# Row maxima split by VectorE before their transposition, which ordinary products make ahead of the values products

## The chip, the core and the metric

The kernel runs on one core of a Trainium2 chip. Its engines are TensorE (PE in the profile; PEld are its weight loads), VectorE (DVE), ScalarE (ACT), GpSimd (POOL) and SyncE (SP), which here issues all transfers. The metric is the device time of one execution in microseconds (us).

## The reference

One transformer block on 2048 positions of width 512, with conditioning: a normalised and modulated input goes through attention with 32 heads of 16 numbers each, then a normalised and modulated sum goes through two dense layers with the Mish function between them.

```python
mod = (_silu(c) @ w_mod).reshape(c.shape[0], 6, 1, -1)
sa, ca, ga, sb, cb, gb = ...
h = _layernorm(x) * (1 + ca) + sa
    qkv = (h @ wqkv) ...                                  # 32 heads of 16
    p = _softmax(einsum("bhqd,bhkd->bhqk", q, k) * 16 ** -0.5)
    o = einsum("bhqk,bhkd->bhqd", p, v)
x = x + ga * (o @ wo)
h = _layernorm(x) * (1 + cb) + sb
x = x + gb * (mish(h @ w1 + b1) @ w2)
```

The softmax is the part that matters here: each score is reduced by the largest one of its row before the exponential.

## The kernel before

**Blocks and steps.** Attention is cut into 32 blocks, n = 0 to 31: 512 queries by 4 heads. A block has 16 steps, each with 128 keys of the 4 heads; the program's step t belongs to block t // 16. In step t, ScalarE needs scores with the keys along the partitions, so the row maxima (along the keys) can't be taken from them. They are found by a second set of products with the queries along the partitions, 20 steps ahead: in step t the maxima of step t + 20 (`PRO`).

**A step.** TensorE makes 4 products for maxima (L471) and 4 for scores (L512), in turn. Each lands in a bank of PSUM of a *ring* of six banks, handed out in order by `ring()`; so the seventh product has to wait until the first one's bank has been read. VectorE reads a maxima product with one reduction (L473, tile `mx`), ScalarE a score product with one exponential (L520, tile `pr`). Products use half of TensorE's rows; the other half makes, beside them, products of the remaining work (L132: projections, and the two dense layers of the query rows that are done already). Then `pv(t - 2)` multiplies the exponentials of two steps before with the values (L540, four products, each in two passes, eight records). Between its exponentials ScalarE also does stages of the dense layers, such as L758, a logarithm of the Mish function.

**The maxima's way.** After the last maxima of a block, in step 16n - 5, `neg_max` reduces them (L482, tile `mm`; each value is written twice, into neighbouring groups of columns). At the end of step 16n - 4, behind that step's values products, `max_rows` takes two neighbouring banks of the ring with `ring(2)`, transposes the two halves of `mm` into them (L490, one transposition for each half of the partitions), and VectorE makes two parts of each value, from PSUM: `mh` (L494) is the value times -1, rounded to TensorE's short type, and `mt` (L495) holds that, or what the rounding left over, according to a column `lows` of 0 and -1. In the middle of the next step SyncE copies `mt` into two further rows of the query tiles `qa` (L501); the key tiles hold ones there, so that the score products come out less their row's maximum.

**Order.** No scheduler moves anything: the order on each engine is the order in which the code of `step` issues. Hooks run work at given half steps; `ats[t]` holds functions that are called at the end of step t, `max_rows` among them. Waits between engines come from what an instruction reads and writes; for the ring they are kept per bank.

Of the kernel before, what the change touches and what calls it, by code (L numbers as in the profile page):

```python
# [8 lines left out]
F32 = mybir.dt.float32  # L9
F32R = mybir.dt.float32r  # L10
AF = mybir.ActivationFunctionType
ALU = mybir.AluOpType
AX = mybir.AxisListType
# [5 lines left out]
def adaln_block(ctx: ExitStack, tc: tile.TileContext, x, wqkv, wo, w1, b1, w2, c, w_mod, out):  # L19
    nc = tc.nc  # L20
    P = 128
# [17 lines left out]
    PRO = 16 + LEAD  # L39
# [7 lines left out]
    out = out[0]  # L47
# [3 lines left out]
    cst = ctx.enter_context(tc.tile_pool(name="cst", bufs=1))  # L51
# [11 lines left out]
    ident = cst.tile([P, P], F32, name="ident")  # L63
# [10 lines left out]
    nc.gpsimd.memset(sel, 0.0)  # L74
    for k in range(DK):
        nc.gpsimd.memset(sel[32 * k:32 * k + 1, :], 1.0)
    lows = cst.tile([P, 1], F32, name="lows")
    nc.vector.tensor_reduce(out=lows[:32], in_=ident[:32, :32].rearrange("p (a v q) -> p v a q", a=4, v=2)[:, 1], op=ALU.add,
                            axis=AX.XY)
    nc.vector.tensor_scalar_mul(lows[:32], lows[:32], -1.0)  # L80
    modc = cst.tile([P, 4, DK], F32, name="modc")
    sil = cst.tile([P, DK], F32, name="sil")
    b1c = cst.tile([P, FT], F32, name="b1c")
# [63 lines left out]
    def ring(w=1):  # L147
        if w == 2 and ring_at[0] % 2:
            ring_at[0] += 1
        b = ring_at[0] % NRING  # L150
        ring_at[0] += w
        return ring_t[:, b, :] if w == 1 else ring_t[:, b:b + 2, :]

    def bank(tag="ms"):
        return ring() if tag == "ring" else ps.tile([P, TB], F32, tag=tag, name="bk", bufs=1)
# [29 lines left out]
    def at(h, f):  # L185

        hooks.setdefault(h, []).append(f)
# [122 lines left out]
    with ExitStack() as es:  # L310
# [69 lines left out]
        for i in range(2):  # L380
            pr.append(ring())
            for k in range(DK):
                nc.tensor.matmul(pr[i][32 * k:32 * k + 32, :], sil[:, k:k + 1].to_broadcast([P, 32]), wma[i][:, k, :],
                                 start=True, stop=True)
# [33 lines left out]
        for tb in range(NB):  # L418
# [4 lines left out]
            parts = []  # L423
# [28 lines left out]
    ap = ctx.enter_context(tc.tile_pool(name="ap", bufs=1, reuse_waits="tile"))  # L452
# [5 lines left out]
        nc.sync.dma_start(t, vscr[n % G])  # L458
        vgs[n] = t

    mxs = {}

    def max_tile(n, j, s, qs, kb):

# [12 lines left out]
    def neg_max(n):  # L477

        mx = mxs.pop(n)
        mm = ap.tile([P, 4, 2, 4], F32, tag="mm", name="mm", bufs=2)  # L480
        twice = bass.AP(tensor=mx.tensor, offset=mx.offset, ap=[list(mx.ap)[0], [16, 4], [0, 2], [4, 4], [1, 4]])
        nc.vector.tensor_reduce(out=mm, in_=twice, op=ALU.max, axis=AX.X)  # L482
        ats.setdefault(16 * n + 16 - PRO, []).append(lambda: max_rows(n, mm))

    def max_rows(n, mm):
        t = ring(2)
        cols = mm.rearrange("p a v q -> p (a v q)")
        for g in range(2):
            r = slice(64 * g, 64 * g + 64)
            nc.tensor.transpose(t[:32, g, :64], cols[r], ident[r, r])  # L490
        pt = t[:32, :, :64]
        mh, mt = [ap.tile([32, P], F32R, tag=n_, name=n_, bufs=1) for n_ in ("mh", "mt")]
        halves = [m.rearrange("p (g q) -> p g q", g=2) for m in (mh, mt)]
        nc.vector.tensor_scalar_mul(halves[0], pt, -1.0)  # L494
        nc.vector.scalar_tensor_tensor(halves[1], halves[0].bitcast(F32), lows[:32], pt, op0=ALU.mult, op1=ALU.subtract)  # L495

        def put():
            for j in range(2):
                for s in range(2):
                    o = (2 * s + j) * 8  # L500
                    nc.sync.dma_start(  # L501
                        qa[(2 * n + j) % NR][64 * s + 48:64 * s + 50, :].rearrange("v (s q) -> v s q", s=4).bitcast(F32),
                        mt[o:o + 8, :].bitcast(F32))
        at(2 * (16 * n + 16 - PRO) + 3, put)
# [27 lines left out]
    def pv(t):  # L532
        if not 0 <= t < T:
            return
        n, kc = divmod(t, 16)
        if kc == 0:
            accs[n] = bank("acc")
        for h in range(4):
            o = (kc * 4 + h) * VW
            nc.tensor.matmul(accs[n][32 * h:32 * h + 32, :], vgs[n][:, o:o + 32], pts.pop((t, h)),  # L540
                             start=(kc == 0), stop=(kc == 15))
        if kc == 15:
            evac(n)

    o_hl = {}
    st, mst = {}, {}

    def evac(n):
        qb, g = divmod(n, G)
# [538 lines left out]
    ats = {}  # L1088
# [47 lines left out]
    def maxima(n, u, s, others):  # L1136

        j, qs = divmod(u, 4)
        return ([max_tile(n, j, s, qs, kb) for kb in range(4 - others)],
                [max_tile(n, j, 1 - s, qs, kb) for kb in range(4 - others, 4)])  # L1140

    def step(t):
        second = t % 2
        n, u = t // 16, t % 16 // 2
        tm = t + PRO
        run_hooks(2 * t)
        if t < 0:

            for i in range(2):
                if tm < 16:  # L1150
                    kb, jq = divmod(2 * tm + i, 8)
                else:
                    jq, kb = tm % 16 // 2, 2 * second + i
                for s in range(2):
                    max_tile(tm // 16, jq // 4, s, jq % 4, kb)()
            if second and tm % 16 == 15:
                neg_max(tm // 16)
            run_hooks(2 * t + 1)
            for f in ats.pop(t, []):
                f()  # L1160
            whole_units(2 * t + 1, CREDIT)
            do_specials(2 * t + 1)
            return
        s = 0 if second else 1
        own, others = ([score(n, j, v, 2 * u + i) for i in range(2) for j in range(2)] for v in (s, 1 - s))
        if not second and 1 < t < T:
            next_part(2 * t)
        part = list(cur["part"])
        f = len(part)
        if t >= T:  # L1170
            if t == T:
                cur["tag"] = "acc"
            run_hooks(2 * t + 1)
            pv(t - 2)
            whole_units(2 * t + 1, 8)
            do_specials(2 * t + 1)
            return
        swap, held = False, None
        if tm < T:
            o = max(0, (8 - f) // 2)  # L1180
            mo, alone = maxima(tm // 16, tm % 16 // 2, s, o)

            mine = [x for p in zip(mo, own) for x in p] + own[len(mo):]
            kinds = [k for p in zip("m" * len(mo), "s" * len(mo)) for k in p] + ["s"] * (len(own) - len(mo))
            swap = 2 <= f <= len(mine) and kinds[f - 1] == "s" and kinds[f - 2] == "m"
            if swap:
                mine[f - 2:f] = mine[f - 1], mine[f - 2]
        else:
            o = max(0, (4 - f) // 2)
            mine = own[o:] if second else own[:4 - o]  # L1190
            alone = others[4 - o:] if second else others[:o]

            m = len(mine)
            if f > m:
                mine = [mine[(i * m) // f] if (i + 1) * m // f > i * m // f else None for i in range(f)]
        beside = part + alone

        def emit(product):
            e = product()
            if cur.pop("want", None):  # L1200
                cur["after"] = e

        ends = second and f and not cur["left"]
        for i in range(max(len(mine), len(beside))):
            if i == len(mine) // 2:
                run_hooks(2 * t + 1)
            if i < f:
                last = i + 1 == f
                if i < len(mine) and mine[i] and not last:
                    if swap and ends and i + 2 == f:  # L1210
                        held = mine[i](True)
                    else:
                        emit(mine[i])
                for m in beside[i]:
                    mm_half(m, second, cur["first"], bool(ends and last and m is beside[i][-1]),
                            cur.pop("after", None))
                    cur["first"] = False
                if last:
                    if ends:
                        cur["fin"](2 * t + 2)  # L1220
                        cur["fin"] = None
                    if held:
                        held()
                    cur["want"] = True
                    if i < len(mine) and mine[i]:
                        emit(mine[i])
            else:
                for x in (*mine[i:i + 1], *beside[i:i + 1]):
                    emit(x)
        if tm < T and tm % 16 == 15:  # L1230
            neg_max(tm // 16)
        do_specials(2 * t + 1)
        pv(t - 2)
        for f in ats.pop(t, []):
            f()

    def do_specials(h):
        if specials and h >= specials[0][0]():
            fin = specials.pop(0)[1]()
            pe_run()  # L1240
            at(h + 1, lambda: fin(h + 1))
# [90 lines left out]
    def run_hooks(h):  # L1332
        while h in hooks:
            for f in hooks.pop(h):
                f()
# [4 lines left out]
    t = T + 2  # L1340
# [32 lines left out]
```

## Time and profile before

| | before |
|---|---|
| median of 3 runs | 1696.65 us (1695.23 to 1700.46) |
| profiled execution | 1693.26 us, span 1691.5 us |
| granted TensorE clock | 0.996 |
| TensorE / VectorE / ScalarE busy | 98% / 85% / 78% |
| transpositions L490 | 64, 228 ns each |
| VectorE L482, L494, L495 | 32 each, 286, 279 and 335 ns |

Busy time is a union of records; a matmul's record reaches to its modelled end, so two that follow each other overlap. In the timeline a row begins with its start and its length in us; what stands in brackets at its end is the idle time of its engine before it, and what ended that. Line numbers are those of the kernel before; from `neg_max` on, the changed kernel's are higher by one (L513 for L512, L521 for L520, L541 for L540), except where the change itself stands.

### The profile page before, as it was taken

What the parts mean: (1) busy time and instruction counts of PE and PEld (TensorE: products, weight loads), DVE (VectorE), ACT (ScalarE), POOL (GpSimd) and SP (SyncE); (2) the same over time, 40 slices, a digit from 0 to 9 for tenths busy, and PEclk for the clock granted to TensorE, in tenths of its full rate; (3) what the DMA queues carried; (4) which work ended last, traced back from release to release, by engine and by line L of the source; (5) the groups of instructions that cost most, each with busy time, mean ns of one, the idle gap of its engine ahead of it and who ended that gap; (6) DMA issues with size and microseconds to landing.
All of it is one profiled execution on the core that took longest, in us unless ns stands there. A gap on an engine that the chain in (4) does not pass through costs nothing.

```text
span 1691.5 us, 32962 instructions
## 1 busy us (share of the span) xinstructions
PE 1660.6 (98%) x12316; PEld 921.7 (54%) x12316; DVE 1429.9 (85%) x2362; ACT 1327.1 (78%) x2559; POOL 898.0 (53%) x906
## 2 busy tenths in 40 slices
PE   6999999999999999999999999999999999999998
PEld 5755665554435455555555555555555555554687
DVE  6898898887998888988888888889888888881577
ACT  6247777777778898888889898888888898889264
POOL 5155215565504388755525498654535597646432
PEclk9999999999999999999999999999999999999999
DMA  7767457777772342434353644334442535332362
GB/s 249 192 224 215 120 159 213 250 226 226 232 210 63 111 123 74 127 80 149 86 133 74 197 105 99 99 109 123 117 103 79 176 95 131 93 107 82 132 218 74
DMA packets 113992, 240.03 MB, mean 142 GB/s; under 512 B 24048, under 2 KB 49648, under 8 KB 107784
## 3 DMA queue, kind: packets, MB, share of 16 engines
q1 hardware_dynamic: 113832, 237.92, 49.6%
q8 instruction: 97, 1.59, 0.4%
q14 instruction: 63, 0.52, 0.1%
HBM read 179.95 MB, written 51.44 MB: 137 GB/s over the span
## 4 chain that ended last, share of the span: by engine, by line
PE 92%; DVE 3%; DMA 2%; ACT 2%; SPq 1%; issue 1%; POOL 0%; DVEq 0%; ACTq 0%; POOLq 0%
PE bk L540 30%; PE ring L471 23%; PE ring L512 22%; PE bk L132 9%; PE bk L126 3%; PE ring L126 3%; PE ring L1074 2%; DVE mx L473 1%; ACT pr L520 1%; DMA xt<-in_A_x 1%; SPq L318 0%; DMA qa<-mt 0%; PE bk L1006 0%; DMA vg<-vscr 0%; PE ring L842 0%
## 5 line engine op out<-in xcount | busy, mean ns | idle before, releaser
L473 DVE TENSOR_REDUCE mx<-ring 128x1 f32<-128x512 f32 x2048 | 1276.1, 684 | 161.5 <-PE bk L132 104.9
L520 ACT ACTIVATE pr<-ring 128x512 f32<-128x512 f32 x2048 | 1090.2, 605 | 232.0 <-PE bk L132 168.8
L471 PE MATMUL ring<-ka,qa 64*128 64x512 f32 x2048 | 778.7, 427 | 0.5
L512 PE MATMUL ring<-qa,ka 64*128 64x512 f32 x2048 | 723.0, 397 | 7.8 <-ACT pr L520 4.6
L471 PEld LDWEIGHTS ring<-ka,qa 64*128 64x128 f32 x2048 | 366.5, 184 | 407.9 <-DVE mx L473 356.2
L540 PE MATMUL bk<-pr,vg 128*32 128x512 f32 x4096 | 545.9, 605 | 0.0
L512 PEld LDWEIGHTS ring<-qa,ka 64*128 64x128 f32 x2048 | 374.1, 184 | 120.8 <-ACT pr L520 35.6
L132 PE MATMUL bk<-h,w 64*128 64x512 f32 x1008 | 280.7, 410 | 0.0
L132 PE MATMUL bk<-w,a_h 64*128 64x512 f32 x576 | 194.8, 417 | 0.6 <-ACT pr L520 0.4
L132 PEld LDWEIGHTS bk<-h,w 64*128 64x128 f32 x1008 | 171.5, 184 | 5.7 <-ACT pr L520 0.4
L540 PEld LDWEIGHTS bk<-pr,vg 128*32 128x32 f32 x4096 | 81.0, 108 | 125.1 <-issue 117.0
L740 POOL TENSOR_SCALAR ee<-hb 128x512 f32<-128x512 f32 x42 | 62.5, 1488 | 96.7 <-ACT hb L734 88.2
L132 PE MATMUL bk<-w,a_l 64*128 64x512 f32 x288 | 113.7, 395 | 0.0
L770 POOL TENSOR_TENSOR ee<-ee,rr 128x512 f32<-128x512 f32 x42 | 53.9, 1284 | 111.6 <-ACT rr L761 111.4
L132 PEld LDWEIGHTS bk<-w,a_h 64*128 64x128 f32 x576 | 95.3, 185 | 5.2 <-ACT pr L520 1.5
L132 PE MATMUL bk<-w,o_hl 64*128 64x512 f32 x288 | 79.7, 409 | 0.0
L98 POOL TENSOR_TENSOR a_l<-hb,a_h 128x512 fp32r<-128x512 f32 x53 | 71.7, 1354 | 4.4
L893 POOL TENSOR_TENSOR y<-yd,y 128x512 f32<-128x512 f32 x40 | 51.4, 1285 | 35.5 <-ACT yd L892 35.3
L754 POOL TENSOR_SCALAR rr<-ee 128x512 f32<-128x512 f32 x42 | 26.1, 622 | 60.0 <-ACT ee L746 59.9
L132 PE MATMUL bk<-h_h,wl 64*128 64x512 f32 x168 | 57.5, 423 | 0.0
L95 POOL TENSOR_SCALAR a_h<-hb 128x512 fp32r<-128x512 f32 x53 | 36.3, 684 | 39.9 <-DVE hb L768 38.3
L774 POOL TENSOR_TENSOR hb<-hb,rr 128x512 f32<-128x512 f32 x42 | 54.5, 1298 | 3.3
(205 smaller groups left out, 1840.9 us busy)
## 6 DMA issues: line engine op xcount, KB each, us to landing
ka<-kscr SPq DMA_DIRECT2D x124, 384.0 KB
w<-w2scr SPq DMA_DIRECT2D x56, 512.0 KB
w<-w1scr SPq DMA_DIRECT2D x46, 512.0 KB
vg<-vscr SPq DMA_DIRECT2D x32, 552.0 KB
qa<-qscr SPq DMA_DIRECT2D x124, 100.0 KB
kscr<-qh SPq DMA_DIRECT2D x16, 512.0 KB
qscr<-qh SPq DMA_DIRECT2D x32, 256.0 KB
hl<-in_B_w SPq DMA_DIRECT2D x28, 256.0 KB
```

Source lines behind the costliest of these rows:

```text
L98: (nc.gpsimd if eng == "p" else nc.vector).tensor_sub(lo, src, hi.bitcast(F32))
L126: nc.tensor.matmul(acc, l, r, start=start, stop=stop)
L132: i = nc.tensor.matmul(acc, l[64 * g:64 * g + 64], r[64 * g:64 * g + 64], start=start, stop=stop)
L471: nc.tensor.matmul(pm, qt[64 * s:64 * s + 64, qs * P:(qs + 1) * P], kt[64 * s:64 * s + 64, kb * TB:(kb + 1) * TB], start=True, stop=True)
L473: return nc.vector.tensor_reduce(out=mxs[n][:, s, 4 * j + qs, kb:kb + 1], in_=pm, op=ALU.max, axis=AX.X)
L512: nc.tensor.matmul(p_, kt[64 * s:64 * s + 64, kc * P:(kc + 1) * P], qt[64 * s:64 * s + 64, :], start=True, stop=True)
L520: e = nc.scalar.activation(pr, p_, AF.Exp, scale=SCALE)
L540: nc.tensor.matmul(accs[n][32 * h:32 * h + 32, :], vgs[n][:, o:o + 32], pts.pop((t, h)), start=(kc == 0), stop=(kc == 15))
L740: nc.gpsimd.tensor_scalar_min(buf("ee", 2), b["hb"], HCAP)
L770: nc.gpsimd.tensor_mul(ee, ee, rr)
L774: nc.gpsimd.tensor_mul(hb, hb, rr)
L893: nc.gpsimd.tensor_add(y[i], yd, y[i])
```

## The change

- `neg_max` reduces to each value once (`mm` is half as large) and splits it at once on VectorE, ahead of the transposition: the value times -1, rounded, and what the rounding left over go into neighbouring groups of columns of a tile `mhl`, whose first 32 columns are used; the other 96 are set to zero once.
- `max_rows` makes two ordinary products of `mhl` (all 128 columns as weights) with a unit matrix `eyes` of the short type, where two transpositions were, and ScalarE copies the result into `mt`; VectorE has nothing more to do with it.
- `max_rows` is called from a list of its own, `ahead`: in step 16n - 4 as before, but in front of `pv(t - 2)`.

```diff
-    lows = cst.tile([P, 1], F32, name="lows")
...
+    eyes = cst.tile([P, P // 2], F32R, name="eyes")
+    for g in range(2):
+        r = slice(64 * g, 64 * g + 64)
+        nc.vector.tensor_copy(eyes[r], ident[r, r])
...
     def neg_max(n):
 
         mx = mxs.pop(n)
-        mm = ap.tile([P, 4, 2, 4], F32, tag="mm", name="mm", bufs=2)
-        twice = bass.AP(tensor=mx.tensor, offset=mx.offset, ap=[list(mx.ap)[0], [16, 4], [0, 2], [4, 4], [1, 4]])
-        nc.vector.tensor_reduce(out=mm, in_=twice, op=ALU.max, axis=AX.X)
-        ats.setdefault(16 * n + 16 - PRO, []).append(lambda: max_rows(n, mm))
-
-    def max_rows(n, mm):
+        mm = ap.tile([P, 4, 4], F32, tag="mm", name="mm", bufs=2)
+        nc.vector.tensor_reduce(out=mm, in_=mx.rearrange("p s (j q) b -> p (s j) q b", j=2), op=ALU.max, axis=AX.X)
+        if "mhl" not in st:
+            st["mhl"] = ap.tile([P, P], F32R, tag="mhl", name="mhl", bufs=1)
+            nc.vector.tensor_scalar_mul(st["mhl"], ident, 0.0)
+        parts = st["mhl"][:, :32].rearrange("p (a v q) -> p a v q", a=4, v=2)
+        nc.vector.tensor_scalar_mul(parts[:, :, 0], mm, -1.0)
+        nc.vector.scalar_tensor_tensor(parts[:, :, 1], parts[:, :, 0].bitcast(F32), -1.0, mm, op0=ALU.mult, op1=ALU.subtract)
+        ahead.setdefault(16 * n + 16 - PRO, []).append(lambda: max_rows(n))
+
+    def max_rows(n):
         t = ring(2)
-        cols = mm.rearrange("p a v q -> p (a v q)")
         for g in range(2):
             r = slice(64 * g, 64 * g + 64)
-            nc.tensor.transpose(t[:32, g, :64], cols[r], ident[r, r])
-        pt = t[:32, :, :64]
-        mh, mt = [ap.tile([32, P], F32R, tag=n_, name=n_, bufs=1) for n_ in ("mh", "mt")]
-        halves = [m.rearrange("p (g q) -> p g q", g=2) for m in (mh, mt)]
-        nc.vector.tensor_scalar_mul(halves[0], pt, -1.0)
-        nc.vector.scalar_tensor_tensor(halves[1], halves[0].bitcast(F32), lows[:32], pt, op0=ALU.mult, op1=ALU.subtract)
+            nc.tensor.matmul(t[:, g, :64], st["mhl"][r], eyes[r], start=True, stop=True)
+        mt = ap.tile([32, P], F32R, tag="mt", name="mt", bufs=1)
+        nc.scalar.copy(mt.rearrange("p (g q) -> p g q", g=2), t[:32, :, :64])
...
         do_specials(2 * t + 1)
+        for f in ahead.pop(t, []):
+            f()
         pv(t - 2)
         for f in ats.pop(t, []):
             f()
```

In the steps before the first (t < 0), which have no values products, `ahead` is called where `ats` was.

TensorE at the end of step 16n - 4, block 12, before: the last three products of the step, the four values products (L540), the two transpositions (L490), and the first products of the next step.

```order
L471 MATMUL ring<-ka_105,qa_107 128x512
L512 MATMUL ring<-qa_109,ka_634 128x512
L471 MATMUL ring<-ka_105,qa_107 128x512
L540 MATMUL bk<-pr_0_1175,vg 32x512
L540 MATMUL bk<-pr_2_1151,vg 32x512
L540 MATMUL bk<-pr_0_1182,vg 32x512
L540 MATMUL bk<-pr_2_1159,vg 32x512
L490 MATMUL ring<-ident,mm 32x64 x2
L471 MATMUL ring<-ka_105,qa_107 128x512
L132 MATMUL bk<-h_5831,w_6934 128x512
```

The same place now (L494 are the two products with the unit matrix, L541 the values products):

```order
L471 MATMUL ring<-ka_105,qa_107 128x512
L513 MATMUL ring<-qa_109,ka_634 128x512
L471 MATMUL ring<-ka_105,qa_107 128x512
L494 MATMUL ring<-eyes,mhl 128x64 x2
L541 MATMUL bk<-pr_0_1177,vg 32x512
L541 MATMUL bk<-pr_2_1153,vg 32x512
L541 MATMUL bk<-pr_0_1184,vg 32x512
L541 MATMUL bk<-pr_2_1161,vg 32x512
L471 MATMUL ring<-ka_105,qa_107 128x512
L132 MATMUL bk<-h_5833,w_6936 128x512
```

The pair has gone past the four values products and follows the step's last product directly; it fills 128 partitions instead of 32.

VectorE around the same border, before: the reduction of `mx` to `mm`, the four maxima of step 16n - 4, then the two parts.

```order
L473 TENSOR_REDUCE mx<-ring 128x1 x20
L482 TENSOR_REDUCE mm<-mx 128x32
L473 TENSOR_REDUCE mx<-ring 128x1 x4
L494 TENSOR_SCALAR mh<-ring 32x128
L495 SCALAR_TENSOR_TENSOR mt<-mh,lows,ring 32x128
L473 TENSOR_REDUCE mx<-ring 128x1 x40
```

The same place now:

```order
L473 TENSOR_REDUCE mx<-ring 128x1 x20
L481 TENSOR_REDUCE mm<-mx 128x16
L486 TENSOR_SCALAR mhl<-mm 128x4x4
L487 SCALAR_TENSOR_TENSOR mhl<-mhl,mm 128x4x4
L473 TENSOR_REDUCE mx<-ring 128x1 x44
```

Three operations now stand in front of the four maxima of step 16n - 4, and none behind them.

ScalarE there, now: the exponentials of step 16n - 4 (L521) with a stage of the Mish function (L759) between the first and the second, the copy into `mt` (L496), and two exponentials of the next step.

```order
L521 ACTIVATE pr_0_1151<-ring 128x512
L759 ACTIVATE rr<-ee,two 128x512
L521 ACTIVATE pr_0_1159<-ring 128x512
L521 ACTIVATE pr_1_1152<-ring 128x512
L521 ACTIVATE pr_1_1160<-ring 128x512
L496 CAST mt<-ring 32x128
L521 ACTIVATE pr_2_1179<-ring 128x512
L521 ACTIVATE pr_2_1186<-ring 128x512
```

The copy is new on this engine and stands behind the step's last exponential; the others have kept their order.

More of the change, by code (lines that the diff above doesn't have):

```diff
@@ L76, in adaln_block @@
         nc.gpsimd.memset(sel[32 * k:32 * k + 1, :], 1.0)
-    lows = cst.tile([P, 1], F32, name="lows")
-    nc.vector.tensor_reduce(out=lows[:32], in_=ident[:32, :32].rearrange("p (a v q) -> p v a q", a=4, v=2)[:, 1], op=ALU.add,
-                            axis=AX.XY)
-    nc.vector.tensor_scalar_mul(lows[:32], lows[:32], -1.0)
+    eyes = cst.tile([P, P // 2], F32R, name="eyes")
+    for g in range(2):
+        r = slice(64 * g, 64 * g + 64)
+        nc.vector.tensor_copy(eyes[r], ident[r, r])
     modc = cst.tile([P, 4, DK], F32, name="modc")
@@ L459, in load_v @@
         vgs[n] = t
-    mxs = {}
+    mxs, st, ahead = {}, {}, {}
     def max_tile(n, j, s, qs, kb):
@@ L545, in adaln_block @@
     o_hl = {}
-    st, mst = {}, {}
+    mst = {}
     def evac(n):
@@ L1158, in step @@
             run_hooks(2 * t + 1)
-            for f in ats.pop(t, []):
+            for f in ahead.pop(t, []) + ats.pop(t, []):
                 f()
```

## The prediction

> **What bounds the kernel now.** I read the page's busy time and chain first, then the length of single steps, then the timeline of one block's border engine by engine. The page, parts 1 and 4:
>
> ```profile
> PE 1660.6 (98%) x12316; PEld 921.7 (54%) x12316; DVE 1429.9 (85%) x2362; ACT 1327.1 (78%) x2559; POOL 898.0 (53%) x906
> PE 92%; DVE 3%; DMA 2%; ACT 2%; SPq 1%; issue 1%; POOL 0%; DVEq 0%; ACTq 0%; POOLq 0%
> ```
>
> TensorE bounds it: 98% busy, 92% of the chain. What counts is the time that TensorE loses or wins per block, and a step is best measured from its first values product (L540) to that of the next step. Three such stretches of block 12's border, from the view that sums windows (length first, after the colon-joined ends):
>
> ```profile
> 651.88:654.72 2.84, 2.84 (x25) 1.53 (x23) 2.79 (x6) 2.07 (x5) 2.76 (x4) 1.00 0.00 0
> 654.72:657.75 3.03, 3.03 (x27) 1.41 (x25) 2.89 (x6) 2.70 (x7) 2.52 (x3) 1.00 0.09 21
> 657.75:660.59 2.84, 2.84 (x24) 1.55 (x23) 2.62 (x6) 2.63 (x6) 1.49 (x1) 1.00 0.13 33
> ```
>
> The middle one holds today's transpositions (L490) and is 0.19 us longer than its neighbours. The step after it is 2.84 again, no shorter: lost time isn't won back. TensorE's timeline there (start, length):
>
> ```profile
> 652.88 0.50 PE L471 MATMUL ring<-ka,qa 64*128 64x512 f32 x1
> 653.22 0.39 PE L512 MATMUL ring<-qa,ka 64*128 64x512 f32 x1
> 653.45 0.39 PE L471 MATMUL ring<-ka,qa 64*128 64x512 f32 x1
> ...
> 654.38 0.40 PE L471 MATMUL ring<-ka,qa 64*128 64x512 f32 x1
> 654.72 1.06 PE L540 MATMUL bk<-pr,vg 128*32 128x512 f32 x8
> 655.71 0.23 PE L490 MATMUL ring<-ident,mm 64*32 64x64 f32 x2
> 655.89 0.49 PE L471 MATMUL ring<-ka,qa 64*128 64x512 f32 x1
> ```
>
> Products follow each other every 0.23 us (653.22 to 653.45), the first one after a load that nothing hides takes 0.34 (652.88 to 653.22), and the values products hold TensorE for 0.99 (654.72 to 655.71). In that 0.99 VectorE and ScalarE empty the ring of six banks; the pair of transpositions comes after it. The weight loads of the following step show where its 0.19 goes, in waits for banks, since VectorE first does the two operations L494 and L495:
>
> ```profile
> 656.38 0.18 PEld L471 LDWEIGHTS ring<-ka,qa 64*128 64x128 f32 x1 [0.19 <-ACT pr L520]
> ...
> 657.31 0.18 PEld L512 LDWEIGHTS ring<-qa,ka 64*128 64x128 f32 x1 [0.17 <-DVE mx L473]
> ```
>
> **The change, part by part.** *Saved.* L494 and L495 leave VectorE and the pair leaves the step 16n-3: it falls to its neighbours' 2.84, 0.19 us less (0.20 below), in 31 blocks.
>
> *The pair in front of the values products.* It takes two neighbouring banks, the fifth and sixth last handed out. A step hands out eight: here maximum 0, score 0, maximum 1, score 1, score 2, maximum 2, score 3, maximum 3. So the pair needs those of maximum 1 and of score 1, whose readers must have ended. Today the 0.99 us of values products lie between; then nothing does. Those two readers and the one ahead of them, in block 12 (VectorE, VectorE, ScalarE):
>
> ```profile
> 653.41 0.69 DVE L473 TENSOR_REDUCE mx<-ring 128x1 f32<-128x512 f32 x1
> 654.02 0.68 DVE L473 TENSOR_REDUCE mx<-ring 128x1 f32<-128x512 f32 x1
> 654.15 0.72 ACT L758 ACTIVATE rr<-ee,two 128x512 f32<-128x512 f32 x1
> 654.78 0.58 ACT L520 ACTIVATE pr<-ring 128x512 f32<-128x512 f32 x1
> ```
>
> Maximum 1 is read by 654.70, but score 1 only by 655.36, since ScalarE had a stage of the second layer (L758) in between: 0.64 us after the values products began today. In such *long* blocks the pair waits for that. I count 16 of them (11 to 16, 19 to 24, 27 to 30), and 13 *short* ones without such a stage. The first and the last of each, values products and the later reader:
>
> ```profile
> 608.84 0.64 PE L540 MATMUL bk<-pr,vg 128*32 128x512 f32 x4
> 608.78 0.59 ACT L520 ACTIVATE pr<-ring 128x512 f32<-128x512 f32 x1
> 1482.78 0.64 PE L540 MATMUL bk<-pr,vg 128*32 128x512 f32 x4
> 1482.72 0.59 ACT L520 ACTIVATE pr<-ring 128x512 f32<-128x512 f32 x1
> ...
> 141.33 0.64 PE L540 MATMUL bk<-pr,vg 128*32 128x512 f32 x4
> 140.63 0.68 DVE L473 TENSOR_REDUCE mx<-ring 128x1 f32<-128x512 f32 x1
> 1299.81 0.64 PE L540 MATMUL bk<-pr,vg 128*32 128x512 f32 x4
> 1299.11 0.68 DVE L473 TENSOR_REDUCE mx<-ring 128x1 f32<-128x512 f32 x1
> ```
>
> Long: 608.78 + 0.59 - 608.84 = 0.53, and the same at 1482.78. Short: 140.63 + 0.68 - 141.33 = -0.02, likewise at 1299.81, so there the bank is free just as the values products begin. I leave two blocks at nothing: block 2, whose step is held up elsewhere, and block 31, whose step has no maxima.
>
> *VectorE's work ahead of the step.* Three operations instead of one stand in front of maximum 0. Rows of their kinds:
>
> ```profile
> L473 DVE TENSOR_REDUCE mx<-ring 128x1 f32<-128x512 f32 x2048 | 1276.1, 684 | 161.5 <-PE bk L132 104.9 <-PE ring L471 55.3 <-PE ring L512 0.3
> L482 DVE TENSOR_REDUCE mm<-mx 128x32 f32<-128x128 f32 x32 | 9.2, 286 | 1.1
> L494 DVE TENSOR_SCALAR mh<-ring 32x128 fp32r<-32x128 f32 x32 | 8.9, 279 | 5.7 <-PE ring L490 2.7
> L495 DVE SCALAR_TENSOR_TENSOR mt<-mh,lows,ring 32x128 fp32r<-32x128 f32 x32 | 10.7, 335 | 1.8 <-DVE mh L494 0.8
> L80 DVE TENSOR_SCALAR lows<-lows 32x1 f32<-32x1 f32 x1 | 0.1, 141 | 0.0
> 653.11 0.28 DVE L482 TENSOR_REDUCE mm<-mx 128x32 f32<-128x128 f32 x1
> ```
>
> (684 - 286) ns for 384 numbers is 1.04 ns each. So the maximum over 64 instead of 128 numbers takes 0.22 us, the product by -1 of 16 numbers 0.16 (between L80's 141 ns and L494's 279), the remainder of 16 numbers 0.335 - 112 x 0.00104 = 0.22 from PSUM, rather 0.19 from SBUF. With two more hand-overs of 0.035: 0.64 against 0.286, 0.35 us later. Nothing covers that: L482 ends at 653.39 and maximum 0 begins at 653.41. In short blocks maximum 1 moves 0.35, and the pair with it; in long ones 0.35 stays under the 0.53 of score 1. Bounds 0.15 (if small operations run in each other's shadow) and 0.45.
>
> *The pair's own time.* No row has an ordinary product over 64 columns. From the start of its load to the values products: 0.11 for a load that nothing hides (0.34 - 0.23), the columns, and 0.12 of changeover (654.38 to 654.72 is 0.34, of which 512 columns hold about 0.22). For the columns:
>
> ```profile
> L132 PE MATMUL bk<-w,a_l 64*128 64x512 f32 x288 | 113.7, 395 | 0.0
> L132 PE MATMUL bk<-wl,h_h 64*128 64x256 f32 x128 | 20.7, 280 | 0.0
> ```
>
> (395 - 280) / 256 = 0.45 ns each, 0.03 us for 64, the two row halves side by side. Together 0.26; below 0.14 if the load hides, above 0.45 (0.34 + 0.11) if it holds TensorE like a product over 512. I take 0.26.
>
> The Trainium skill, "TensorE: Matmul & The Clock Gate", section Terms, has the transpose mode 4 times faster for FP32 than ordinary products; if that held for this rounded type too, the pair would stream 0.12 us instead of 0.03. Those two rows speak against it, one pass at 0.45 ns per column. The Trainium skill, "Perfetto Trace Analysis", section Transposes, asks outright for a transpose "as opposed to a standard matmul"; no run here shows it yet.
>
> *The sum.* A bank that was waited for is used some 0.05 us after its reader's end (L495 ends at 656.67 in the row below, and the load that waits for it starts at 656.72).
>
> ```profile
> 656.33 0.34 DVE L495 SCALAR_TENSOR_TENSOR mt<-mh,lows,ring 32x128 fp32r<-32x128 f32 x1
> 656.72 0.18 PEld L512 LDWEIGHTS ring<-qa,ka 64*128 64x128 f32 x1
> ```
>
> Long: 0.53 + 0.05 + 0.26 = 0.84 later, less 0.20 saved: +0.64, 16 times, 10.2 us. Short: -0.02 + 0.35 + 0.05 + 0.26 = 0.64, less 0.20: +0.44, 13 times, 5.7. Behind the pair on TensorE stand the four values products and the whole next step, so the delay is the kernel's. Off the other way: at one place TensorE waits long for SyncE's copies of the transposed rows anyway (chain of waits):
>
> ```profile
> 382.29 6.10 DMA qa<-mt
> ```
>
> Its queue is held by transfers of its own, so part of what six blocks lost before it is swallowed; I take 1 us of at most 2.6. Sum +14.9.
>
> *At nothing.* ScalarE's copy to mt replaces L495: it stands behind score 3, ends about when L495 does today, and the next exponentials wait for products that come 1 us after the values products begin. So SyncE's four transfers per block stay where they are, and no other queue is passed. Block 0 has no values products yet. The unit matrix and the zeros are made once, a few tenths at the start.
>
> The profiled execution took 1693.26 us (span 1691.5), 3.4 below the median of 1696.65. 1693.26 + 14.9 = 1708.2 for an execution like it; against the median, 1711.6: 1711.5 is the forecast. With the pair's own bounds (-0.12 or +0.19, 29 times), VectorE's (-0.20 or +0.10, 13 times) and the swallowed part (0 to 2.6) it would be 1704 to 1719.
>
> **The rivals.** *The pair is slow as an ordinary product:* it holds TensorE for 0.35 to 0.45, by a rounded type that streams small products slowly or by a change of type in front of the values products. For it: the loads of L540 stand still for 0.24 us in front of every step's values products, for no shown reason:
>
> ```profile
> 654.72 0.16 PEld L540 LDWEIGHTS bk<-pr,vg 128*32 128x32 f32 x8 [0.24 <-issue]
> ```
>
> Against: the 0.45 ns per column. 29 x 0.09 to 0.19 more: 1714 to 1717. Chance 0.2. It is the side on which the two pages of the Trainium skill named above stand.
>
> *No change:* the banks are free when TensorE arrives, because in the changed order ScalarE's extra stage or the maxima fall elsewhere. Then the pair costs 0.14 to 0.26 and 0.20 is saved: 1695 to 1699. Against: the stage L758 stands between the same two exponentials in both orders. Chance 0.08.
>
> *Faster:* the delay of the values products is made good. While TensorE waits, VectorE and ScalarE empty all banks; if the next step held as much waiting as was lost, it would shrink by that and only the saving remained, 31 x 0.20 = 6.2: 1690.5. It decides from the point where a normal step holds 0.6 us of waits. Against: the steps at 2.84 run at 0.23 per product, and the one after the 3.03 is not shorter. Chance 0.1.
>
> *Worse:* one late step makes later ones late (a transfer that misses its turn, ScalarE's copy in front of the next exponentials), another 0.3 per block: 1721. Chance 0.07.
>
> **How the numbers follow.** The forecast keeps 0.55. 0.3% (5 us) is about what a measurement of this kernel can tell from no change: faster 0.1, same 0.08, slower 0.82. The range goes from 1700 to 1720: it leaves out the faster case, most of the no-change case and the worst.
>
> **What would show it.** In the changed profile: steps 16n-4 longer by about 0.84 and 0.64, steps 16n-3 at 2.84; the pair's loads waiting for L473 or for the exponentials (L521 there) rather than for nothing; long blocks dearer than short ones; values products some 0.26 behind the pair's load. Wrong, if the pair's load starts 0.1 us behind the last product, if the step after it is shorter than 2.84, or if VectorE's two new operations together take under 0.15.

## The result, and the profile after

| | before | after |
|---|---|---|
| median (lowest to highest) | 1697.62 us (1695.23 to 1700.46, 4 runs) | 1717.58 us (1711.6 to 1722.86, 4 runs) |
| profiled execution, span | 1693.26, 1691.5 us | 1711.6, 1709.8 us |
| granted TensorE clock | 0.996 | 0.999 |

The changed kernel takes 1.0121 times as long [1.0099, 1.0142]: slower by 20 us. (The median before is over one run more than in the table above.) The page of the profile after, parts 1 and 4:

```profile
PE 1672.4 (98%) x12316; PEld 935.3 (55%) x12316; DVE 1431.9 (84%) x2363; ACT 1331.4 (78%) x2591; POOL 898.3 (53%) x906
PE 88%; DVE 6%; DMA 2%; ACT 2%; issue 1%; SPq 0%; POOL 0%; DVEq 0%; ACTq 0%
```

TensorE's share of the chain fell from 92% to 88%, and VectorE's rose from 3% to 6%: TensorE now waits for reductions. Where it does so is read from steps again, from one values product to the next (now L541). The view that sums windows, of the changed kernel, two rows each (step 16n - 4, then 16n - 3) for block 5 (short), block 16 (long) and block 12 (long):

```profile
331.54:334.87 3.33, 3.30 (x27) 1.67 (x25) 3.23 (x8) 3.05 (x8) 1.42 (x2) 1.00 0.98 322
334.87:337.72 2.85, 2.85 (x24) 1.53 (x23) 2.23 (x5) 1.68 (x6) 2.68 (x4) 1.00 0.68 261
842.94:846.58 3.64, 3.60 (x27) 1.83 (x25) 3.54 (x9) 2.88 (x7) 0.62 (x1) 1.00 0.02 5
846.58:849.42 2.84, 2.84 (x24) 1.54 (x23) 1.93 (x5) 1.88 (x6) 2.67 (x4) 1.00 0.01 1
656.60:661.48 4.88, 3.45 (x27) 1.65 (x25) 4.78 (x8) 3.46 (x8) 4.71 (x6) 1.00 0.03 6
661.48:664.32 2.84, 2.84 (x25) 1.54 (x23) 2.23 (x5) 1.52 (x5) 0.44 (x1) 1.00 0.21 46
```

All three steps 16n - 3 are at 2.84 or 2.85, as forecast. The steps 16n - 4, 2.84 before, are 3.33 and 3.64, and in block 12 4.88, which no part of the forecast has.

Block 16 goes the forecast way. Its timeline: first what VectorE does ahead of maximum 0, then ScalarE around score 1, then TensorE's loads and products up to the values products.

```profile
844.17 0.22 DVE L481 TENSOR_REDUCE mm<-mx 128x16 f32<-128x64 f32 x1
844.42 0.17 DVE L486 TENSOR_SCALAR mhl<-mm 128x16 fp32r<-128x16 f32 x1
844.63 0.17 DVE L487 SCALAR_TENSOR_TENSOR mhl<-mhl,mm 128x16 fp32r<-128x16 f32 x1
844.73 1.28 DVE L473 TENSOR_REDUCE mx<-ring 128x1 f32<-128x512 f32 x2
845.19 0.62 ACT L762 ACTIVATE rr<-rr 128x512 f32<-128x512 f32 x1
845.71 0.59 ACT L521 ACTIVATE pr<-ring 128x512 f32<-128x512 f32 x1
846.06 0.48 PEld L494 LDWEIGHTS ring<-eyes,mhl 64*128 64x128 f32 x2 [0.34 <-DVE mx L473]
846.06 0.59 PE L494 MATMUL ring<-eyes,mhl 64*128 64x64 f32 x2
846.58 1.07 PE L541 MATMUL bk<-pr,vg 128*32 128x512 f32 x8
```

Maximum 1 ends at 844.73 + 1.28 = 846.01, and the first product of the pair starts 0.05 later. The second waits for score 1, which ScalarE, busy with the Mish stage (L762) until 845.81, ends at 845.71 + 0.59 = 846.30. The values products follow 0.28 after that.

In block 12 something else came first. VectorE, GpSimd and TensorE's loads there:

```profile
657.82 0.22 DVE L481 TENSOR_REDUCE mm<-mx 128x16 f32<-128x64 f32 x1
658.07 0.69 DVE L486 TENSOR_SCALAR mhl<-mm 128x16 fp32r<-128x16 f32 x1
658.80 1.20 DVE L487 SCALAR_TENSOR_TENSOR mhl<-mhl,mm 128x16 fp32r<-128x16 f32 x1
657.45 1.29 POOL L756 TENSOR_TENSOR ee<-ee,rr 128x512 f32<-128x512 f32 x1
658.69 1.28 POOL L98 TENSOR_TENSOR o_hl<-od,o_hl 128x512 fp32r<-128x512 f32 x1
660.65 0.18 PEld L513 LDWEIGHTS ring<-qa,ka 64*128 64x128 f32 x1 [1.84 <-DVE mx L473]
```

The same two operations on 16 numbers take 0.69 and 1.20 us where block 16 has 0.17. The first ends at 658.76, 0.02 after GpSimd's L756; the second at 660.00, 0.03 after GpSimd's L98. TensorE meanwhile stands still for 1.84 us, waiting for maxima that VectorE has not begun. The view of the tile `mhl`, with the shortest, middle and longest of the 32, and the same for the reduction `mm` and the copy to `mt`:

```profile
L486 DVE TENSOR_SCALAR mhl<-mm x32: 174/374/1187, 95.8 to 1545.3; 128x16 fp32r<-128x16 f32 x32
L487 DVE SCALAR_TENSOR_TENSOR mhl<-mhl,mm x32: 174/176/1202, 96.0 to 1545.6; 128x16 fp32r<-128x16 f32 x32
L481 DVE TENSOR_REDUCE mm<-mx x32: 219/220/222, 95.4 to 1545.1; 128x16 f32<-128x64 f32 x32
L496 ACT CAST mt<-ring x32: 238/240/255, 97.0 to 1547.9; 32x128 fp32r<-32x128 f32 x32
```

The reduction and the copy hardly vary; the two new operations do, in 19 of the 32 blocks, by 10.75 us in all. The trace ties this to GpSimd row by row. Of the 32 rows of L486, 18 began while an operation of GpSimd was running; each of these ended 0.03 us after that operation, and the other 14 took 174 to 176 ns. Of L487, seven began so: five ended 0.02 to 0.03 us after GpSimd's operation, two were let through (176 and 199 ns), and the other 25 took 174 to 178 ns.

The operations they replace never met this, though GpSimd was running when 26 of the 32 rows of L494 and 25 of L495 began. Their views, of the kernel before:

```profile
L494 DVE TENSOR_SCALAR mh<-ring x32: 269/279/281, 97.2 to 1529.1; 32x128 fp32r<-32x128 f32 x32
L495 DVE SCALAR_TENSOR_TENSOR mt<-mh,lows,ring x32: 333/335/339, 97.6 to 1529.4; 32x128 fp32r<-32x128 f32 x32
```

Step by step against the profile before, the span's 18.3 us come out of these parts: steps 16n - 4 give +26.7, steps 16n - 3 give -7.2, the few steps that transfers hold up -2.9 (step 96 alone -3.1), the start, up to the first values product, +1.8, and all the others about -0.1.

### The profile page after: what moved, and what is told of

It is laid out like the page before. It is cut to its first block, busy times and chain, and to the rows that moved or that the text cites. A ratio compares the mean times of both kernels' runs of the same rounds, so it can differ in the third digit from the quotient of the medians.

```text
span 1709.8 us, 33051 instructions
## 1 busy us (share of the span) xinstructions
PE 1672.4 (98%) x12316; PEld 935.3 (55%) x12316; DVE 1431.9 (84%) x2363; ACT 1331.4 (78%) x2591; POOL 898.3 (53%) x906
## 4 chain that ended last, share of the span: by engine, by line
PE 88%; DVE 6%; DMA 2%; ACT 2%; issue 1%; SPq 0%; POOL 0%; DVEq 0%; ACTq 0%
PE bk L541 28%; PE ring L471 22%; PE ring L513 19%; PE bk L132 9%; DVE mx L473 3%; PE bk L126 3%; PE ring L126 3%; PE ring L1075 1%; ACT pr L521 1%; PE ring L494 1%; DMA wma<-in_w_mod 1%; DMA ka<-kscr 1%; DVE mhl L486 0%; DMA qa<-mt 0%; DVE hf L374 0%
## 5 line engine op out<-in xcount | busy, mean ns | idle before, releaser
L521 ACT ACTIVATE pr<-ring 128x512 f32<-128x512 f32 x2048 | 1091.0, 605 | 244.9 <-PE bk L132 182.1
L541 PE MATMUL bk<-pr,vg 128*32 128x512 f32 x4096 | 545.1, 604 | 0.0
L541 PEld LDWEIGHTS bk<-pr,vg 128*32 128x32 f32 x4096 | 80.9, 108 | 118.6 <-issue 109.3
L98 POOL TENSOR_TENSOR a_l<-hb,a_h 128x512 fp32r<-128x512 f32 x53 | 71.7, 1354 | 4.4
```

Source lines behind the costliest of these rows:

```text
L98: (nc.gpsimd if eng == "p" else nc.vector).tensor_sub(lo, src, hi.bitcast(F32))
L521: e = nc.scalar.activation(pr, p_, AF.Exp, scale=SCALE)
```

## The experiments

Changes in steps, below, are those of each profiled execution against the profile before; medians and ratios are against the kernel before on the same chip. "Place" is the call in front of the values products.

**The change with the pair behind the values products.** VectorE's split, the ordinary products and ScalarE's copy stay.

```diff
 # against the changed kernel
-        ahead.setdefault(16 * n + 16 - PRO, []).append(lambda: max_rows(n))
+        ats.setdefault(16 * n + 16 - PRO, []).append(lambda: max_rows(n))
...
-        for f in ahead.pop(t, []):
-            f()
         pv(t - 2)
```

> The changed kernel with one thing undone: the pair of products with the unit matrix stands behind the values products again. Theory (three causes: the pair waits for banks in front of the values products; three VectorE operations ahead of the step's maxima, 0.35 us; two of these held up while GpSimd works): only the first goes. Steps 16n-4 still 0.25 longer where VectorE isn't held up, 0.5 where it is held up by 0.2 to 0.3, and above 1.2 in blocks 4, 12, 20 and 28; steps 16n-3 at 2.90. Sum +8 to +12 us on the kernel before. Rival (the place is everything): the time of the kernel before or less, -3 to +1 us.

It took 1709.49 us, ratio 1.0062 [1.0046, 1.0078], +11.3. Its windows, block 12 and block 16 (both steps):

```profile
661.65:666.17 4.52, 3.17 (x25) 1.47 (x23) 4.42 (x8) 3.18 (x7) 4.35 (x6) 1.00 0.00 0
846.44:849.45 3.01, 3.01 (x24) 1.46 (x22) 2.91 (x8) 2.25 (x6) 0.00 (x0) 1.00 0.00 0
849.45:852.39 2.94, 2.94 (x26) 1.64 (x24) 2.55 (x6) 2.65 (x7) 2.77 (x3) 1.00 0.02 6
```

Block 16's step is 0.19 longer than before where I expected 0.25; the pair behind costs its next step some 0.10 more than the place does (2.94 against 2.84). Block 12 keeps +1.68: its long stall does not hang on the place. So about half of the loss stays when the place is undone. In sum the border steps (16n - 4 and 16n - 3 of every block) lost 10.3 us; transfer waits, which sit in other steps here, added 4.5, and I read no more from the total than its size.

**The place alone.** The kernel before, transpositions, `mh` and `mt` as they were, `max_rows` called in front of `pv`.

```diff
 # against the kernel before
-        ats.setdefault(16 * n + 16 - PRO, []).append(lambda: max_rows(n, mm))
+        ahead.setdefault(16 * n + 16 - PRO, []).append(lambda: max_rows(n, mm))
...
+        for f in ahead.pop(t, []):
+            f()
         pv(t - 2)
```

> The kernel before with one thing changed: its pair of transpositions stands in front of the values products; the parts are still made by VectorE from PSUM afterwards. Theory: the bank wait alone, long blocks 0.53 + 0.05 + 0.17 longer in step 16n-4 and 0.19 shorter in the next (+0.56), short blocks about 0; sum +7 to +10 us. Rival (VectorE's work and the port are everything): within 2 us of the kernel before.

1704.86 us, 1.0037 [1.0021, 1.0054], +6.7: just below the 7 to 10 expected. Steps 16n - 4 of block 16 (long) and 25 (short):

```profile
840.05:843.62 3.57, 3.26 (x26) 1.71 (x24) 3.52 (x7) 2.81 (x7) 0.55 (x1) 1.00 0.02 5
1257.91:1260.97 3.06, 3.06 (x27) 1.66 (x25) 3.00 (x6) 2.79 (x7) 1.28 (x1) 1.00 0.01 3
```

Long blocks lose mostly 0.74, short ones mostly 0.21, and most save 0.19 in the next step. Blocks 12, 20 and 28 lose 0.83 to 0.84: without the two operations on VectorE their long stall is gone.

**The split on GpSimd.** If VectorE's 0.35 us matter, moving the two operations to GpSimd should give them back.

```diff
 # against the changed kernel
-        nc.vector.tensor_scalar_mul(parts[:, :, 0], mm, -1.0)
-        nc.vector.scalar_tensor_tensor(parts[:, :, 1], ...)
+        hi_copy("p", parts[:, :, 0], mm)
+        lo_sub("p", parts[:, :, 1], mm, parts[:, :, 0])
...
-        nc.scalar.copy(mt..., t[:32, :, :64])
+        nc.scalar.activation(mt..., t[:32, :, :64], AF.Identity, scale=-1.0)
```

> The changed kernel with the two operations that split the maxima on GpSimd instead of VectorE (signs turned by ScalarE's copy). Theory: the bank wait and the pair stay (long blocks +0.61 over both steps, all 16 alike), VectorE's delay and its hold-ups go (short blocks +0.06); sum +8 to +12 us, blocks 4, 12, 20, 28 without their 2 us. If GpSimd gets to its two operations too late, the pair waits for it instead, and the sum is 15 or more. Rival (the place is everything): as the changed kernel, +18 us.

1743.06 us, 1.0263 [1.0248, 1.0278], +44.9: the late case of the expectation, and far worse than its 15. The view of waits, then block 5's window, then GpSimd's timeline there:

```profile
PEld ring L494 <- POOL mhl L98: 37.1, 13, 6.7
334.08:342.79 8.71, 3.25 (x26) 1.81 (x25) 3.88 (x7) 3.55 (x8) 5.79 (x8) 0.85 0.78 238
336.66 1.27 POOL L658 TENSOR_TENSOR hl<-hl,gate 128x512 f32<-128x512 f32 x1 [4.07 <-DMA hl<-in_A_wo]
...
341.88 0.20 POOL L95 TENSOR_SCALAR mhl<-mm 128x16 fp32r<-128x16 f32 x1
342.17 0.22 POOL L98 TENSOR_TENSOR mhl<-mm,mhl 128x16 fp32r<-128x16 f32 x1
```

The two operations are as short there (0.20 and 0.22), but they stand in GpSimd's queue behind five longer ones, the first of which waited 4.07 us for a transfer. TensorE waited 37.1 us for them in 13 places. In the blocks where GpSimd was in time, short ones lost mostly 0.33 to 0.36 and long ones 0.80.

**The same with two idle reductions on VectorE,** to put back the time but not the dependence:

```diff
 # against the split on GpSimd
+        for o in (32, 48):
+            nc.vector.tensor_reduce(out=st["mhl"][:, o:o + 16], in_=mm..., op=ALU.max, axis=AX.X)
```

> The kernel with the split on GpSimd, and on VectorE two reductions of the same 16 numbers, whose results nobody uses, where the split stood: VectorE's delay of about 0.35 without the two forms of operation that were held up. Theory: short blocks +0.4 over both steps as in the undisturbed short blocks of the changed kernel, long ones as with the split on GpSimd; 4 to 5 us above that kernel, and the rest of the changed kernel's loss (6 to 8 us) is the hold-ups. Rival (a longer queue on VectorE is all, and the hold-ups cost nothing): as the changed kernel, +18 us.

1744.65 us, 1.0273 [1.0254, 1.0292]. The totals of the two can't be told apart, since GpSimd's lateness rules both. By steps, where GpSimd was in time, most short blocks lose 0.51 to 0.53, 0.17 more than without the reductions, and long ones 0.80 as before. So time put in front of maximum 0 counts in most short blocks and not in long ones. It does not count in the short blocks 10, 18 and 26 either, which lose the same with and without the reductions. The reductions (view of the tile `mhl`):

```profile
L489 DVE TENSOR_REDUCE mhl<-mm x64: 157/165/172, 95.9 to 1576.0; 128x16 fp32r<-128x16 f32 x64
```

None of the 64 was held up, though they stand where L486 and L487 stood, and 34 of them began while GpSimd was running.

**Reductions in place of the two operations.** So the hold-up may belong to the form of the operation. Here VectorE makes the rounded maximum and a zero by two reductions.

```diff
 # against the changed kernel
-        nc.vector.tensor_scalar_mul(parts[:, :, 0], mm, -1.0)
-        nc.vector.scalar_tensor_tensor(parts[:, :, 1], ...)
+        nc.vector.tensor_reduce(out=parts[:, :, 0], in_=mm.unsqueeze(3), op=ALU.max, axis=AX.X)
+        nc.vector.tensor_reduce(out=parts[:, :, 1], in_=zero.unsqueeze(3), op=ALU.max, axis=AX.X)
...
-        nc.scalar.copy(mt..., t[:32, :, :64])
+        nc.scalar.activation(mt..., t[:32, :, :64], AF.Identity, scale=-1.0)
```

> The changed kernel with the two splitting operations replaced by two reductions at the same place (the rounded maximum, and zeros in place of what the rounding left over, which this kernel leaves out). VectorE has three operations there as before, but only of the form whose time never varied (L481, 219 to 222 ns). Theory (VectorE's L486 and L487 are held up while GpSimd works): all short blocks +0.49 in step 16n-4, all long ones +0.80 to +0.87, blocks 1, 4, 6, 12, 20, 28 among them; 6 to 9 us below the changed kernel, +10 to +13 us on the kernel before. Rival (small operations on VectorE vary anyway, or TensorE's waits in those blocks have another cause): blocks 4, 12, 20, 28 keep their 2 us, and the time is that of the changed kernel.

1706.47 us, 1.0064 [1.005, 1.0079], +10.0, where the change has 1.0121. The two reductions by the view of the tile, then steps 16n - 4 of blocks 12, 16 and 25:

```profile
L487 DVE TENSOR_REDUCE mhl<-mm x32: 169/170/172, 96.7 to 1539.2; 128x16 fp32r<-128x16 f32 x32
L488 DVE TENSOR_REDUCE mhl<-mhl x32: 157/159/161, 96.8 to 1539.3; 128x16 fp32r<-128x16 f32 x32
654.70:658.44 3.74, 3.48 (x27) 1.83 (x25) 3.67 (x9) 2.97 (x7) 3.66 (x5) 1.00 0.00 0
839.92:843.56 3.64, 3.47 (x27) 1.83 (x25) 3.57 (x9) 2.88 (x7) 0.63 (x1) 1.00 0.02 5
1258.30:1261.50 3.20, 3.17 (x26) 1.65 (x24) 3.13 (x8) 2.94 (x7) 1.29 (x1) 1.00 0.00 0
```

No hold-up is left, though GpSimd was running when 19 of the 32 rows of each began, and block 12 is 3.74 instead of 4.88, with GpSimd still busy for 3.66 us of it. Blocks 4 and 6, +1.85 and +1.10 in the changed kernel, are at +0.37 and +0.36. Only block 1 keeps its +1.5, which I had expected to go. The timeline of this kernel shows why, in TensorE's wait there:

```profile
142.77 0.47 PE L471 MATMUL ring<-ka,qa 64*128 64x512 f32 x1 [1.21 <-DMA ka<-kscr]
```

It is a wait for keys, not for VectorE. (In the changed kernel block 1 has both: 0.76 us for the same keys, and the longest L486, 1.19.) Two things differ at once: these reductions also overlap, so that maximum 0 begins 0.42 us after L481 instead of 0.56. That 0.14 is at most 1.8 us over 13 short blocks; the steps 16n - 4 gain 7.3 in sum.

**Transpositions in the changed kernel.** The split and the place stay; only the ordinary products go.

```diff
 # against the changed kernel
-            nc.tensor.matmul(t[:, g, :64], st["mhl"][r], eyes[r], start=True, stop=True)
+            nc.tensor.transpose(t[:32, g, :64], st["mhl"][r, :32].bitcast(F32), ident[r, r])
```

> The changed kernel with transpositions of its 32 columns in place of the ordinary products with all 128. Theory (a load of 32 columns is 0.09 shorter, the columns themselves cost 0.03 either way): pair to values products 0.17 instead of 0.23, 1 to 2 us below the changed kernel. Rival (the ordinary product is the loss, a transposition is much cheaper): 0.10 or less from the pair's load to the values products, 4 us or more below the changed kernel.

1714.42 us, 1.0108 [1.0095, 1.0122]; the interval meets that of the change, so the total decides nothing. The steps do: undisturbed blocks lose 0.05 to 0.07 less than in the changed kernel. The loads at block 25's border, first the changed kernel, then this one:

```profile
1266.23 0.19 PEld L494 LDWEIGHTS ring<-eyes,mhl 64*128 64x128 f32 x2 [0.34 <-DVE mx L473]
1266.45 0.16 PEld L541 LDWEIGHTS bk<-pr,vg 128*32 128x32 f32 x8
```

```profile
1270.83 0.09 PEld L494 LDWEIGHTS ring<-ident,mhl 64*32 64x32 f32 x2 [0.34 <-DVE mx L473]
1270.99 0.16 PEld L541 LDWEIGHTS bk<-pr,vg 128*32 128x32 f32 x8
```

From the pair's load to the values products it is 0.22 us with ordinary products and 0.16 with transpositions. The load itself, of 128 columns instead of 32, takes 0.19 instead of 0.09. The Trainium skill, "Perfetto Trace Analysis", section Transposes, prefers a transpose to a standard matmul; the steps agree, and put 0.06 us per block on it, some 1.9 us of the 20. But the kind of product and the width of its weights change together here. No run makes ordinary products with 32 columns, so which of the two costs the 0.06 is not shown.

**A version without the remainder.** If the rounded maximum is enough, the kernel before can drop both VectorE operations where it has them, behind the values products, and ScalarE can make `mt` in one.

```diff
 # against the kernel before
-    nc.vector.tensor_scalar_mul(lows[:32], lows[:32], -1.0)
+    nc.vector.tensor_scalar_add(lows[:32], lows[:32], -1.0)
...
-        nc.vector.tensor_scalar_mul(halves[0], pt, -1.0)
-        nc.vector.scalar_tensor_tensor(halves[1], halves[0].bitcast(F32), lows[:32], pt, op0=ALU.mult, op1=ALU.subtract)
+        nc.scalar.activation(mt..., t[:32, :, :64], AF.Identity, scale=lows[:32])
```

> The kernel before, its transpositions behind the values products, but instead of two operations on VectorE one copy on ScalarE with a factor for each partition: -1 in the rows of the rounded maximum, 0 in those of the remainder, which this kernel leaves out (the softmax doesn't depend on the number subtracted, as long as it is the same for a whole row). Theory (step 16n-3 is 0.19 longer today because VectorE's two operations make maxima and banks late): steps 16n-3 at 2.88 to 2.94 instead of 3.03, steps 16n-4 as they are; 3 to 5 us faster than the kernel before, ratio 0.997 to 0.998. Rival (the pair itself costs the 0.19): no change, 0.999 to 1.001.

1692.95 us (1689.54 to 1697.34, 11 runs), 0.9981 [0.997, 0.9992]: 3.5 us faster than the kernel before, and faster than both; a gain below the 0.3% of the prediction, but the interval leaves out 1. Steps 16n - 3 of block 16 and block 12:

```profile
836.03:838.93 2.90, 2.90 (x26) 1.50 (x24) 2.48 (x5) 2.77 (x8) 2.55 (x3) 1.00 0.00 0
653.70:656.73 3.03, 3.03 (x27) 1.54 (x25) 2.50 (x5) 2.92 (x8) 2.52 (x3) 1.00 0.13 30
```

Short blocks save 0.17 to 0.19 and long ones mostly 0.11 to 0.13. Blocks 12, 20 and 28 save nothing: their step stays at 3.03.

## Why the prediction was right, and where it was not

Direction and place were right: the loss sits in the steps 16n - 4, the saving in the steps 16n - 3. By its own steps:

- **Saved 0.20 in 31 blocks:** the quoted steps fell to 2.84 and 2.85, mostly by 0.19. Right.
- **The pair waits for its two banks, long blocks for score 1:** shown in block 16 (0.05 after the reader's end, as taken) and by the place alone. Long blocks were to lose 0.84 and lost 0.80 to 0.81. Right.
- **The pair's own time, 0.26:** 0.22 to 0.23. With transpositions it is 0.16, so 0.06 is for ordinary products with 128 columns as weights. So the rival of the slow ordinary product was wrong, although its 1714 to 1717 lies at the measured time.
- **VectorE's three operations, 0.35 later, counted in full in short blocks and not at all in long ones:** undisturbed they take 0.22, 0.17 and 0.17 us, which with the hand-overs is the 0.35. But maximum 0 does not wait for the last of them to end: in block 16 it begins at 844.73, and L487 ends at 844.80. From the start of L481 to maximum 0 it is 0.56 (844.17 to 844.73), where the kernel before has 0.30 from L482 (653.11 to 653.41). So maximum 0 came 0.26 later, or 0.24 to 0.26 in the undisturbed short blocks 3, 5 and 7. The prediction's own sum with that size and the pair's 0.23, -0.02 + 0.25 + 0.05 + 0.23 = 0.51, is what these three lost: 0.49 instead of 0.64. The mechanism was right and the term was 0.1 too large, 1.8 us over 13 blocks together with the pair's 0.03. And "nothing covers that", read in block 12, does not hold everywhere: in blocks 10, 18 and 26 VectorE reaches L481 0.4 to 0.5 us earlier in the step, maximum 0 begins as before, and they lost only 0.39, 0.27 and 0.27. In long blocks it stayed under the wait for score 1, as taken.
- **VectorE's upper bound, 0.45: this is the step that failed.** The prediction took the length of the operations from rows of their kinds and asked what stands on VectorE only. Their operands lie in SBUF, where L494 had its one and L495 one of its two in PSUM, and beside GpSimd's work the pair of them took up to 1.9 us. The rows of L494 and L495 could have warned of nothing: GpSimd ran beside most of them, and they never varied. (That this is for the operand's place, and not for the shape, 32x128 against 128x16, no run separates.) In blocks 12, 20 and 28 the steps lost 2.02 to 2.05, where with reductions they lost 0.90; block 4 lost 1.85 and block 6 1.10 where undisturbed short ones lose 0.49. These five make 5.4 us. Blocks 9, 17 and 25 add 0.25 each. In long blocks smaller hold-ups of 0.2 to 0.3 stay under the wait for score 1, as in blocks 11, 19 and 27 (0.81).
- **"No other queue is passed":** true of the order, and not enough: GpSimd held VectorE up without an instruction or a semaphore of the change on it. Reductions at the same place were never held up (157 to 172 ns), and with them the ratio fell from 1.0121 to 1.0064, about half of the loss. The Trainium skill, "SBUF — State Buffer", section Who interferes with whom, names a port pair that GpSimd and VectorE lock for a whole instruction, and has it that a `tensor_scalar` or an operation with two SBUF inputs can meet it, a `tensor_reduce` on trn2 never. The rows agree on each of the three forms, except that two of L487 were let through (above).
- **Swallowed, 1 of at most 2.6:** the step with SyncE's wait, 96, gave back 3.1, and the steps with transfer waits in sum 2.9. The direction was right, the bound too low. But such waits sit in different steps in each execution, as the chain of the changed kernel shows:

```profile
132.83 9.13 DMA ka<-kscr
433.01 5.38 DMA qa<-mt
489.34 4.82 DMA sm<-ot
```

- **At nothing (ScalarE's copy, SyncE):** the copy takes 0.24 us in all 32 blocks and the step behind it is 2.84. Right.
- **The other rivals:** no next step shrank below its neighbours' length, 2.83 to 2.86 in most blocks (2.74 in blocks 8 and 10, where the step ahead was 2.73 before), which was the sign of the faster one. The worse one was to come from transfers or ScalarE's copy making later steps late; the extra microseconds came from a third place.

In sum, the span's 18.3 us come out of the +14.9 so: -0.4 in long blocks (0.61 net instead of 0.64), -1.8 if all short blocks had lost 0.49, -1.9 for transfers, +1.8 at the start and -0.1 in all the rest. The other +5.8 are the hold-ups and block 1's keys, less what blocks 10, 18 and 26 did not lose and what single blocks saved beyond 0.19.

That the time came inside the range is in part luck. The terms that the prediction had gave about 4 us less than it took them for (0.4, 1.8 and 1.9 above), and the hold-ups, which were in none of its terms, put more than that back.

The start is not explained. The first values product came 1.8 to 7.0 us later in all six kernels that make the two parts ahead of the pair, and 0.5 later and 1.0 earlier in the two that don't (the place alone, and the one without the remainder), against "a few tenths" in the prediction. So part of it may belong to the change, and with one profile of each it can't be told from scatter. Also open is why the four runs of the changed kernel lie 11 us apart where those of the kernel before lie 5.

The parts on the chip: the place alone 0.37%, the split with ordinary products behind the values products 0.62%, both, as in the change, 1.21%, of which reductions in place of the two operations take off 0.57%. The first two add up to 0.99%; the intervals are too wide to say whether the 0.22% between is more than scatter.

## What to carry to other kernels

Work that needs no fresh bank or tile (here the values products) is the cover under which others empty banks: what is put in front of it has to find its own banks free, and the reader that ends last sets the price, with the new instruction's length on top. When a small operation moves to another operand memory, ask which engine shares its way there: a row of the same kind from PSUM says nothing of it from SBUF beside a busy GpSimd, and a reduction at the same place was not held up at all. A short instruction handed to an idle-looking engine comes when that engine's queue lets it, so read its queue at that point and not its busy share.

## What the runs showed of the hardware that I had not expected

- VectorE's operations on 16 numbers per partition from SBUF took 174 ns alone and up to 1187 and 1202 ns beside GpSimd, ending 0.02 to 0.03 us after GpSimd's operation. L486 was held up in exactly the 18 blocks where an operation of GpSimd was running when it began. The Trainium skill, "SBUF — State Buffer", section "SBUF: two separate sides", has the loser blocked for the whole instruction; that is how the held-up rows read.
- GpSimd, 53% busy in the changed kernel, served two operations of 0.2 us so late, when the split was put on it, that TensorE waited for them up to 6.7 us. In block 5's long step (8.71 us) the granted clock was 0.85, where it is 1.00 in every other window shown.
- The loads of the ordinary pair, of 128 weight columns, took 0.19 us against 0.09 for the transpositions' 32; of that, 0.06 us per block reached the values products.
